# Attention with a gated unit: q and k transposes ahead of each burst's scores, casts and loads further ahead, last tokens in another burst, diagonals on VectorE

## The chip, the cores and the metric

The kernel runs on one core of a Trainium2 chip. The metric is the device time of one launch in microseconds (us), as the median of several runs; smaller is better. A profiled execution gives a span (first to last instruction) and a time of its own, which is a little longer than the span.

## The reference

Batch 8, 8 heads, 576 tokens, head dimension 64; all inputs are float32. Causal attention works in blocks of 64 tokens, and its output goes through a gated unit with a causal convolution of five taps:

```python
scores = scale * np.matmul(q, k.transpose(0, 1, 3, 2))      # scale = 1/8
scores = np.where(block_i >= block_j, scores, -1000000000.0)
attn = exp(scores - max); attn = attn / (sum + 1e-09)
x = matmul(attn, v), heads side by side                       # [8, 576, 512]
gate = sigmoid(sum over k of conv_w[k] * x shifted by 4 - k tokens)
out = (gate * (x @ w_val)) @ w_out                            # [8, 576, 512] float32
```

## The kernel before

Two heads of a batch make a pair; there are 32 pairs, four to a batch. The 576 tokens of a head are 512 "first" tokens and 64 "last" tokens (the tails). The order of all instructions is written out by hand (a manual schedule), so each engine works through its queue in the order of the program. The names in the profile are those of the tiles.

**Per pair.** `load_qk` (L101) puts q and k of a pair into the tile `kqst` through the queue of SyncE (SP); a pool `ld` of four buffers holds them. `cast_qk` (L134) makes float16 of them (tile `ckq`, four buffers), for all but the first pairs as one operation on GpSimd (POOL, L139). `trans` (L155) turns them with 16 small TensorE transposes into two PSUM banks (`ps_tr`, L163), and four copies of 128x256 carry these to `kT` and `qT` (L170, L173): three on VectorE (DVE) and one on ScalarE (ACT) from pair 8 on, two and two before. Column block 8 of `kT` is a copy of block 6 (L179). `scores` (L200) makes one of three chunks of a pair in a PSUM tile `S` of two banks, of which there are two; `exps` (L230) takes the exponential on ScalarE into `pt` (L232, 1.03 us), and for chunks 1 and 2 a copy and memsets on GpSimd follow (L235, L239, L242). `pv` (L256) multiplies with v (`ps_o`), and VectorE divides by the sums (L282, L284). `xt_pair` (L289) transposes the result (`ps_xt`, L296).

**The tails.** The q and k of a batch's last tokens are loaded for all 8 heads (`load_tails`, L114), cast (`cast_tails`, L144, tile `ct`), and transposed by `trans_tails` (L183, `ps_tt`) into `kX` and `qX`, which the scores of all four pairs of that batch read.

**The gated unit.** `gate` (L300) makes the convolution as TensorE products with diagonal matrices (`ps_gate`; `make_diag` L570 builds the 16 diagonals), with the last taps on VectorE (L312, and L327 in `end_gates`, L323) and a tanh on ScalarE (L319, L330). `val` (L333, `ps_val`) and `out_tile` (L356, `ps_out`, evicted by ScalarE at L367) are spread over the iterations by `filler` (L590), which takes work units from a list by fixed costs.

**PSUM.** Besides the two score tiles there are four banks, given out in turn (`bank`, L92) to `ps_tr`, `ps_tt`, `ps_o`, `ps_xt`, `ps_gate`, `ps_val`, `ps_out`. A piece of TensorE work that gets a bank waits until the piece four before it has been evicted.

**The loop** (L613) takes two pairs at a time, a and z = a + 1, in 16 iterations. Each has three bursts, each with two score chunks: (a,0) and (a,1); then (a,2) and (z,0); then (z,1) and (z,2). After the first burst come pv of the pair before and filler, after the second pv(a, part 0), after the third pv(a, part 1); gates and filler stand behind each. `j` is 0 or 2: an iteration with j = 0 has the first two pairs of a batch, j = 2 the last two. Bursts two and three also transpose pairs a + 2 and z + 2: in `burst` (L244) the scores come first, then `trans`, then the exponentials, with the last of the copies (the one on ScalarE) behind the first exponential:

```python
made = [(p, c, scores(p, c)) for p, c in chunks]
left = trans(ahead) if ahead < NP else None
if tails_of < B:
    trans_tails(tails_of)
```

Pair a + 2 is cast behind the first burst and pair z + 2 behind the second; each is transposed one burst later. The tails of the next batch are loaded at the start of an iteration with j = 0, cast behind the second burst of the one with j = 2, and transposed in its third burst.

Of the kernel before, what the change touches and what calls it, by code (L numbers as in the profile page):

```python
# [16 lines left out]
def kernel(  # L17
# [10 lines left out]
    nc = tc.nc  # L28
    fp32 = mybir.dt.float32
    fp16 = mybir.dt.float16  # L30
    AF = mybir.ActivationFunctionType
    ALU = mybir.AluOpType
    PSUM = bass.MemoryType.PSUM

    B, H, SEQ, D = q.shape
    NP = B * H // 2
# [11 lines left out]
    def const(shape, dtype, name):  # L48
        return cpool.tile(shape, dtype, tag=name, name=name)

    ident = const([128, 128], fp32, "ident")
    ident16 = const([128, 128], fp16, "ident16")
# [3 lines left out]
    convT = const([128, 4, 5], fp32, "convT")  # L56
    diag = const([128, 4, 4, 128], fp16, "diag")
# [19 lines left out]
    xts = [const([128, 4, PAD + SEQ], fp16, f"xt{i}") for i in range(2)]  # L77

    fast = ExitStack()
    ld = fast.enter_context(tc.tile_pool(name="ld", bufs=4))  # L80
    ldt = fast.enter_context(tc.tile_pool(name="ldt", bufs=2))
    wk = fast.enter_context(tc.tile_pool(name="wk", bufs=3))
    mo = fast.enter_context(tc.tile_pool(name="mo", bufs=6))
# [8 lines left out]
    def bank(name, dtype=fp32):  # L92
        return psM.tile([128, 512] if dtype == fp32 else [128, 1024], dtype,
                        tag="misc", name=name)
# [3 lines left out]
    FIRST = 8  # L98
# [21 lines left out]
    def load_v(p):  # L120
        b = p // PPB
        vs[p] = ld.tile([128, 2, 4, 64], fp32, tag="v", name="vst")
        for e in range(2):
            h = 2 * (p % PPB) + e
            nc.sync.dma_start(
                out=vs[p][:, e, :, :],
                in_=v[b, h, 0:512, :].rearrange("(t p) d -> p t d", p=128))
# [6 lines left out]
    def cast_qk(p, hows):  # L134
        t = c16[p] = wk.tile([128, 2, 4, 2, 64], fp16, tag="ckq", name="ckq", bufs=4)
        src = raw.pop(p)
        to = t[:, :, :, :, :].rearrange("p i t e d -> p i e t d")
        if len(hows) == 1:
            hows[0](out=to, in_=src[:, :, :, :, :])  # L139
        else:  # L140
            for i, how in enumerate(hows):
                how(out=to[:, i], in_=src[:, i, :, :, :])  # L142

    def cast_tails(b, how):  # L144
        t = tails[b] = wk.tile([128, 8, 64], fp16, tag="ct", name="ct", bufs=2)
        how(out=t[:, :, :], in_=tails32.pop(b)[:, :, :])

    def cast_v(p):
        nc.gpsimd.tensor_copy(out=ves[p % NV][:, :, :, 0:64], in_=vs.pop(p)[:, :, :, :])  # L149
# [5 lines left out]
    def trans(p):  # L155
        src = c16.pop(p)
        ps = [bank("ps_tr", fp16) for _ in range(2)]
        for i in range(2):
            for t in range(4):
                for r in range(2):  # L160
                    h = slice(64 * r, 64 * r + 64)
                    a = 256 * i + 64 * t
                    nc.tensor.transpose(out=ps[r][:, a:a + 64], in_=src[h, i, t, :, :],  # L163
                                        identity=ident16[h, h])

        def evict(i, r, copy):
            dst = (kTs[p % NT][:, 0:8, :], qTs[p % NT][:, :, :])[i]
            got = ps[r][:, 256 * i:256 * i + 256]
            if p < FIRST:
                copy(out=dst[:, 4 * r:4 * r + 4, :].rearrange("p n (s t) -> p (n s) t", t=4),  # L170
                     in_=got.rearrange("p (t s) -> p s t", t=4))
            else:
                copy(out=dst[:, r:8:2, :], in_=got.rearrange("p (t x) -> p t x", x=64))  # L173

        K = kTs[p % NT]
        evict(0, 0, nc.vector.tensor_copy)
        evict(0, 1, nc.vector.tensor_copy)
        copy = nc.vector.tensor_copy if p < FIRST else nc.gpsimd.tensor_copy
        copy(out=K[:, 8, :], in_=K[:, 6, :])  # L179
        evict(1, 0, nc.scalar.copy if p < FIRST else nc.vector.tensor_copy)  # L180
        return lambda: evict(1, 1, nc.scalar.copy)

    def trans_tails(b):  # L183
        src = tails.pop(b)
# [15 lines left out]
    def scores(p, c):  # L200
        ps = psS.tile([128, 2, 512], fp32, tag="S", name="S")
        b, j = divmod(p, PPB)
        K, Q = kTs[p % NT], qTs[p % NT][:, :, :].rearrange("p n x -> p (n x)")
        kx, qx = kXs[b % 2][:, j, :, :], qXs[b % 2][:, j, :]

        def group(off, lhsT, rhs, start=True, stop=True):
            n = rhs.shape[-1]
            for e in range(2):
                r = slice(64 * e, 64 * e + 64)
                mm(out=ps[:, e, off:off + n], lhsT=lhsT[r, :, :], rhs=rhs[r, :],  # L210
                   start=start, stop=stop)

        if c == 0:
            group(0, K[:, 0:2, :], Q[:, 0:512])
        elif c == 1:
            group(0, K[:, 2:4, :], Q[:, 128:512])

            group(384, K[:, 8:10, :], Q[:, 384:448], stop=False)
            group(384, kx, qx, start=False)
            group(448, K[:, 6:8, :], Q[:, 448:512])  # L220
        else:
            group(0, K[:, 4:6, :], Q[:, 256:512])
            for tt in range(4):
                group(256 + 64 * tt, K[:, 2 * tt:2 * tt + 2, :], qx)
        return ps
# [16 lines left out]
            nc.gpsimd.memset(seg[:, :, :, 0:64], 0.0)  # L242

    def burst(chunks, ahead=NP, tails_of=B):  # L244
        made = [(p, c, scores(p, c)) for p, c in chunks]
        left = trans(ahead) if ahead < NP else None
        if tails_of < B:
            trans_tails(tails_of)
        for p, c, s in made:
            exps(p, c, s)  # L250
            if left:
                left()
                left = None
        end_gates()

    def pv(p, part):  # L256
# [294 lines left out]
    load_v(1)  # L551
    load_qk(3)
    load_v(2)

    def load_weights():
        nc.gpsimd.dma_start(out=w_val_sb[:, :, :],
# [12 lines left out]

    def make_diag(g):  # L570
        for j in range(4):
            nc.scalar.activation(out=diag[:, g, j, :], in_=ident16[:, :], func=AF.Copy, bias=0.0,
                                 scale=convT[:, g, j:j + 1])

# [23 lines left out]

    pool = nc.gpsimd.tensor_copy
    cast_qk(0, (nc.vector.tensor_copy, nc.scalar.copy))
    cast_tails(0, nc.vector.tensor_copy)
    cast_qk(1, (nc.vector.tensor_copy, pool))
    cast_v(0)
    cast_vtails(0)
    cast_qk(2, (pool,))
    cast_v(1)
    trans(0)()
    trans_tails(0)  # L610
    trans(1)()

    for a in range(0, NP, 2):  # L613
        z = a + 1
        b, j = divmod(a, PPB)
        if a + 4 < NP:
            load_qk(a + 4)
        if a + 3 < NP:
            load_v(a + 3)
        if j == 0 and b + 1 < B:  # L620
            load_vtails(b + 1)
            load_tails(b + 1)
        flush()

        burst([(a, 0), (a, 1)])
        if 0 < a < NP - 2:
            cast_qk(a + 2, (pool,))
        if a:
            pv(z - 2, 0)
            filler(0.6)  # L630
            pv(z - 2, 1)
            xt_pair(a - 2)
        if a == 4:

            xt_pair(z - 2)
            for p in (a - 2, z - 2):
                gate(p, 0)
                gate(p, 1)
            end_gates()
            vals, outs = units(0)  # L640
            for _, work in vals:
                work()
            fill.extend(outs)
            weights[:] = [8.0]
            spent[0] = 0.0
        if a == 0:
            transpose_conv()
            make_diag(0)
            make_diag(1)
        filler(1.4)  # L650

        burst([(a, 2), (z, 0)], a + 2)
        if z + 4 < NP:
            load_qk(z + 4)
        if z + 3 < NP:
            load_v(z + 3)
        flush()
        if a and a != 4:
            xt_pair(z - 2)
        if z + 2 < NP:  # L660
            cast_qk(z + 2, (pool,))
        if a + 2 < NP:
            cast_v(a + 2)
        if j == 2 and b + 1 < B:
            cast_tails(b + 1, pool)
        pv(a, 0)
        if a > 4:
            if j == 0:
                vals, outs = units(b - 1)
                fill.extend(vals + outs)  # L670
                weights[:] = [8.0]
                spent[0] = 0.0
        if a == 0:
            load_weights()
            make_diag(2)
        filler(0.6)
        if a and a != 4:
            gate(a - 2, 0)
            gate(a - 2, 1)
        filler(0.6)  # L680

        burst([(z, 1), (z, 2)], z + 2, b + 1 if j == 2 else B)
        if z + 2 < NP:
            cast_v(z + 2)
        pv(a, 1)
        if j == 2 and b + 1 < B:
            cast_vtails(b + 1)
        if a == 0:
            make_diag(3)
        filler(0.4)  # L690
        if a and a != 4:
            gate(z - 2, 0)
            gate(z - 2, 1)
        filler(0.4)
# [62 lines left out]
```

## Time and profile before

| | |
|---|---|
| median of 3 runs | 222.28 us (222.24 to 222.92) |
| the profiled execution | 220.88 us, span 218.8 us |
| TensorE busy | 184.5 us (84%) |
| VectorE / ScalarE / GpSimd busy | 157.4 / 150.2 / 99.4 us |
| mean granted TensorE clock | 0.983 |

In the timeline a row gives the start and the length in us, the engine, the line and the operation with its tiles; in square brackets stands how long the engine had been idle before it and what ended that. "PEld" is the weight load of TensorE, "SPq" the queue of SyncE, on which loads and stores are issued.

### The profile page before, as it was taken

What the parts mean: (1) busy time and instruction counts of PE and PEld (TensorE: products, weight loads), DVE (VectorE), ACT (ScalarE), POOL (GpSimd) and SP (SyncE); (2) the same over time, 40 slices, a digit from 0 to 9 for tenths busy, and PEclk for the clock granted to TensorE, in tenths of its full rate; (3) what the DMA queues carried; (4) which work ended last, traced back from release to release, by engine and by line L of the source; (5) the groups of instructions that cost most, each with busy time, mean ns of one, the idle gap of its engine ahead of it and who ended that gap; (6) DMA issues with size and microseconds to landing.
All of it is one profiled execution on the core that took longest, in us unless ns stands there. A gap on an engine that the chain in (4) does not pass through costs nothing.

```text
span 218.8 us, 7511 instructions
## 1 busy us (share of the span) xinstructions
PE 184.5 (84%) x2946; PEld 128.4 (59%) x2946; DVE 157.4 (72%) x457; ACT 150.2 (69%) x227; POOL 99.4 (45%) x216
## 2 busy tenths in 40 slices
PE   1447889959688998999899989998999899998990
PEld 0335666745556756576567655675577566765740
DVE  3633468844687969698869876998699686989840
ACT  3299487269784868786887669768866887875420
POOL 4257446033745654647464554637455545410000
PEclk9999999988999999999999999999999999999996
DMA  5999998993988977997798887978799312001233
GB/s 154 266 290 151 230 293 170 198 229 100 232 194 206 234 163 210 251 209 160 184 264 208 183 236 181 236 172 202 198 265 213 100 65 100 0 37 62 100 135 115
DMA packets 107794, 39.36 MB, mean 180 GB/s; under 512 B 98021, under 2 KB 103141, under 8 KB 107754
## 3 DMA queue, kind: packets, MB, share of 16 engines
q1 hardware_dynamic: 106554, 37.51, 69.4%
q0 software_dynamic: 1056, 1.05, 3.2%
q8 instruction: 25, 0.41, 0.8%
q10 hardware_dynamic: 144, 0.26, 0.3%
q14 instruction: 15, 0.12, 0.2%
HBM read 30.42 MB, written 9.44 MB: 182 GB/s over the span
## 4 chain that ended last, share of the span: by engine, by line
PE 46%; DVE 16%; ACT 10%; issue 7%; DMA 7%; POOL 6%; SPq 6%; POOLq 0%; DVEq 0%; ACTq 0%
PE ps_val L43 10%; PE ps_out L43 10%; PE ps_gate L43 8%; PE ps_o L43 7%; PE S L43 6%; ACT pt L232 5%; DVE kT L173 4%; PE ps_tr L163 3%; DMA kqst<-in_k_dram 3%; POOL ckq L139 3%; DVE xn L284 3%; DVE th L327 3%; SPq L111 3%; DMA kqst<-in_q_dram 3%; ACT qT L170 2%
## 5 line engine op out<-in xcount | busy, mean ns | idle before, releaser
L232 ACT ACTIVATE pt<-S 128x1024 f16<-128x1024 f32 x96 | 96.6, 1027 | 21.8 <-PE S L43 21.4
L43 PE MATMUL ps_o<-ve,pt 128*128 128x65 f16 x896 | 39.8, 198 | 4.3 <-DVE qT L173 3.3
L43 PE MATMUL ps_val<-xt,w_val 128*128 128x288 f16 x256 | 37.6, 286 | 2.3 <-DVE qT L173 1.7
L43 PEld LDWEIGHTS <-pt 128*128 128x128 f16 x896 | 34.5, 101 | 7.5 <-DVE qT L173 3.9
L43 PE MATMUL ps_out<-w_out,gv 128*128 128x512 f16 x144 | 36.4, 385 | 0.8 <-DVE qT L173 0.8
L43 PE MATMUL S<-qT,kT 64*128 64x64 f16 (+3 forms) x320 | 31.8, 288 | 6.1 <-ACT pt L232 6.1
L367 ACT ACTIVATE ob<-ps_out 128x512 f32<-128x512 f32 x34 | 20.3, 598 | 20.1 <-PE ps_out L43 19.1
L284 DVE TENSOR_TENSOR xn<-ps_o,rinv 128x256 f16<-128x256 f32 x64 | 31.4, 491 | 2.2
L312 DVE SCALAR_TENSOR_TENSOR th<-xt,convT,ps_gate 128x288 f32<-128x288 f16 x64 | 30.2, 508 | 3.1 <-PE ps_gate L43 3.0
L43 PEld LDWEIGHTS <-kT 64*128 64x128 f16 x576 | 18.5, 98 | 23.7 <-issue 21.4
L139 POOL CAST ckq<-kqst 128x1024 f16<-128x1024 f32 x30 | 31.1, 1038 | 2.5 <-DMA kqst<-in_q_dram 0.7
L43 PE MATMUL ps_gate<-xt,diag 128*128 128x288 f16 x204 | 31.1, 291 | 0.9 <-DVE qT L173 0.8
L235 POOL COPY pd<-pt 64x128 f16<-64x128 f16 x32 | 12.8, 399 | 38.0 <-ACT pt L232 32.8
L43 PEld LDWEIGHTS <-w_val 128*128 128x128 f16 x256 | 23.0, 97 | 9.7 <-DVE qT L173 2.4
L344 DVE SCALAR_TENSOR_TENSOR gv<-th,ps_val 128x288 f16<-128x288 f32 x64 | 27.7, 449 | 1.0 <-PE ps_val L43 0.3
L173 DVE COPY kT<-ps_tr 128x256 f16<-128x256 f16 x48 | 11.7, 286 | 19.5 <-PE ps_tr L163 19.4
L43 PEld LDWEIGHTS <-diag 128*128 128x128 f16 x204 | 19.2, 99 | 7.3 <-DVE qT L173 1.2
L163 PE MATMUL ps_tr<-ident,ckq 64*128 64x64 f16 x512 | 14.5, 199 | 10.3 <-DVE ckq L142 4.1
L327 DVE SCALAR_TENSOR_TENSOR th<-xt,convT,th 128x576 f32<-128x576 f16 x26 | 21.2, 815 | 0.3
L43 PEld LDWEIGHTS <-gv 128*128 128x128 f16 x144 | 13.4, 99 | 12.7 <-DVE qT L173 1.2
L149 POOL CAST ve<-vst 128x512 f16<-128x512 f32 x32 | 19.6, 614 | 2.3 <-DMA vst<-in_v_dram 1.3
L242 POOL MEMSET pt<- 64x256 f16 x32 | 9.8, 306 | 22.3 <-ACT pt L232 20.6
(61 smaller groups left out, 204.4 us busy)
## 6 DMA issues: line engine op xcount, KB each, us to landing
out_dram<-ob SPq DMA_DIRECT2D x35, 256.0 KB, 3.3
vst<-in_v_dram SPq DMA_DIRECT2D x64, 128.0 KB, 3.2
kqst<-in_k_dram SPq DMA_DIRECT2D x48, 128.0 KB, 3.0
kqst<-in_q_dram SPq DMA_DIRECT2D x48, 128.0 KB, 3.2
kqst<-in_k_dram SPq DMA_DIRECT2D x8, 256.0 KB, 5.0
kqst<-in_q_dram SPq DMA_DIRECT2D x8, 256.0 KB, 5.2
t<-in_k_dram SPq DMA_DIRECT2D x8, 128.0 KB, 3.7
t<-in_q_dram SPq DMA_DIRECT2D x8, 128.0 KB, 3.6
```

The costliest lines, as they stand in the source:

```text
L43: nc.tensor.matmul(out=out, lhsT=lhsT, rhs=rhs, start=start, stop=stop, skip_group_check=True)
L139: hows[0](out=to, in_=src[:, :, :, :, :])
L149: nc.gpsimd.tensor_copy(out=ves[p % NV][:, :, :, 0:64], in_=vs.pop(p)[:, :, :, :])
L163: nc.tensor.transpose(out=ps[r][:, a:a + 64], in_=src[h, i, t, :, :], identity=ident16[h, h])
L173: copy(out=dst[:, r:8:2, :], in_=got.rearrange("p (t x) -> p t x", x=64))
L232: nc.scalar.activation(out=pt[:, :, 512 * c:512 * c + 512], in_=ps[:, :, :], func=AF.Exp, bias=0.0, scale=0.125)
L235: nc.gpsimd.tensor_copy(out=pds[p % NPT][64:128, 0:128].rearrange("p (e x) -> p e x", e=2), in_=pt[64:128, :, COL[3]:COL[3] + 64])
L284: nc.vector.tensor_tensor(out=x.rearrange("p c (e d) -> p (c e) d", e=2), in0=og[:, :, 0:64], in1=ri.to_broadcast([128, n, 64]), op=ALU.mult)
L312: nc.vector.scalar_tensor_tensor(out=th, in0=xts[b % 2][:, g, s0 + 4:s0 + 4 + HALF], scalar=convT[:, g, 4:5], in1=gp[:, 0:HALF], op0=ALU.m ...
L327: nc.vector.scalar_tensor_tensor(out=th, in0=xts[b % 2][:, g, 3:3 + SEQ], scalar=convT[:, g, 3:4], in1=th, op0=ALU.mult, op1=ALU.add)
L344: nc.vector.scalar_tensor_tensor(out=gvs[u][:, g, SEQ * bi + s0:SEQ * bi + s0 + HALF], in0=ths[b][:, g, s0:s0 + HALF], scalar=1.0, in1=vp[ ...
L367: nc.scalar.activation(out=ob[:, :], in_=ps[:, :], func=AF.Copy, bias=0.0, scale=0.5)
```

## The change

`trans` is issued ahead of the burst's scores, and all four copies out of it follow at once (no copy is kept for after the first exponential); for pairs from 8 on VectorE's order is k, q, k. The copy of block 6 of `kT` becomes a function of its own, `copy_key`, on GpSimd from pair 2 on, issued behind the burst. Pair z + 2 is cast behind the first burst, pair a + 4 behind the third. Loads run one pair further ahead, with five buffers. The tails of the next batch are cast behind the third burst of the iteration with j = 0, and transposed at the head of the first burst of the iteration with j = 2. The 16 diagonals are made on VectorE. In the prologue the first pair is transposed right behind its cast, the second pair behind the first burst.

```diff
-    ld = fast.enter_context(tc.tile_pool(name="ld", bufs=4))
+    ld = fast.enter_context(tc.tile_pool(name="ld", bufs=5))
...
+        evict(0, 0, nc.vector.tensor_copy)
+        evict(1, 0, nc.scalar.copy if p < FIRST else nc.vector.tensor_copy)
+        evict(0, 1, nc.vector.tensor_copy)
+        evict(1, 1, nc.scalar.copy)
+
+    def copy_key(p, how):
         K = kTs[p % NT]
-        evict(0, 0, nc.vector.tensor_copy)
-        evict(0, 1, nc.vector.tensor_copy)
-        copy = nc.vector.tensor_copy if p < FIRST else nc.gpsimd.tensor_copy
-        copy(out=K[:, 8, :], in_=K[:, 6, :])
-        evict(1, 0, nc.scalar.copy if p < FIRST else nc.vector.tensor_copy)
-        return lambda: evict(1, 1, nc.scalar.copy)
+        how(out=K[:, 8, :], in_=K[:, 6, :])
...
     def burst(chunks, ahead=NP, tails_of=B):
-        made = [(p, c, scores(p, c)) for p, c in chunks]
-        left = trans(ahead) if ahead < NP else None
+        if ahead < NP:
+            trans(ahead)
         if tails_of < B:
             trans_tails(tails_of)
-        for p, c, s in made:
+        for p, c, s in [(p, c, scores(p, c)) for p, c in chunks]:
             exps(p, c, s)
-            if left:
-                left()
-                left = None
         end_gates()
...
+    load_qk(4)
...
-            nc.scalar.activation(out=diag[:, g, j, :], in_=ident16[:, :], func=AF.Copy, bias=0.0,
-                                 scale=convT[:, g, j:j + 1])
+            nc.vector.tensor_scalar(out=diag[:, g, j, :], in0=ident16[:, :],
+                                    scalar1=convT[:, g, j:j + 1], scalar2=None, op0=ALU.mult)
...
     cast_qk(0, (nc.vector.tensor_copy, nc.scalar.copy))
+    trans(0)
+    copy_key(0, nc.vector.tensor_copy)
     cast_tails(0, nc.vector.tensor_copy)
+    trans_tails(0)
     cast_qk(1, (nc.vector.tensor_copy, pool))
+    cast_qk(2, (pool,))
     cast_v(0)
     cast_vtails(0)
-    cast_qk(2, (pool,))
-    cast_v(1)
-    trans(0)()
-    trans_tails(0)
-    trans(1)()
...
-        if a + 4 < NP:
-            load_qk(a + 4)
+        if a + 5 < NP:
+            load_qk(a + 5)
...
-        burst([(a, 0), (a, 1)])
-        if 0 < a < NP - 2:
-            cast_qk(a + 2, (pool,))
+        burst([(a, 0), (a, 1)], tails_of=b + 1 if j == 2 else B)
+        if a == 0:
+            trans(1)
+            copy_key(1, nc.vector.tensor_copy)
+        if z + 2 < NP:
+            cast_qk(z + 2, (pool,))
+        if a == 0:
+            cast_v(1)
...
         burst([(a, 2), (z, 0)], a + 2)
-        if z + 4 < NP:
-            load_qk(z + 4)
+        if a + 6 < NP:
+            load_qk(a + 6)
...
-        if z + 2 < NP:
-            cast_qk(z + 2, (pool,))
         if a + 2 < NP:
             cast_v(a + 2)
-        if j == 2 and b + 1 < B:
-            cast_tails(b + 1, pool)
+            copy_key(a + 2, pool)
         pv(a, 0)
...
-        burst([(z, 1), (z, 2)], z + 2, b + 1 if j == 2 else B)
+        burst([(z, 1), (z, 2)], z + 2)
+        if a + 4 < NP:
+            cast_qk(a + 4, (pool,))
         if z + 2 < NP:
             cast_v(z + 2)
+            copy_key(z + 2, pool)
+        if j == 0 and b + 1 < B:
+            cast_tails(b + 1, pool)
         pv(a, 1)
```

## The prediction

> **What bounds the kernel now.** I read the page's slices first, then the waits of TensorE, then the timeline of one period, engine by engine. The slices:
>
> ```profile
> PE   1447889959688998999899989998999899998990
> PEclk9999999988999999999999999999999999999996
> ```
>
> TensorE is short of work at the start and around 46 us, full behind that. What it waits for (total, times, longest):
>
> ```profile
> PE S L43 <- ACT pt L232: 6.1, 9, 1.6
> ...
> PE ps_o L43 <- DVE qT L173: 3.3, 5, 0.7
> PE ps_tr L163 <- POOL ckq L139: 3.2, 3, 1.3
> ```
>
> The first and third fall before 69.4 us. The second is a PSUM bank: work behind the transposes waits until the bank of `ps_tr` is evicted. With the same wait of `ps_val`, `ps_gate` and `ps_out` (1.7, 0.8, 0.8 us) it makes 6.6 us in all. From 69 us the kernel repeats every 46.0 us (two batches); the stretches by engine (length, then busy PE, PEld, DVE, ACT, POOL, then the clock):
>
> ```profile
> 44.10:47.50 3.40, 1.08 (x33) 0.83 (x30) 1.45 (x5) 2.70 (x5) 1.07 (x2) 1.00 0.97 223
> 47.50:50.90 3.40, 3.40 (x53) 2.50 (x53) 1.69 (x5) 1.97 (x4) 1.38 (x4) 0.53 0.76 167
> 64.50:67.90 3.40, 1.81 (x33) 1.26 (x33) 1.85 (x8) 2.15 (x4) 2.30 (x6) 1.00 0.99 253
> 92.57:138.58 46.01, 43.00 (x734) 29.89 (x736) 37.63 (x109) 35.21 (x49) 25.18 (x52) 1.00 0.84 208
> ```
>
> So a period leaves TensorE 3.0 us idle, all that any reordering can win there. GpSimd is busy for only 25 of 46 us, but in series. Its row around the tails' cast (`ct`):
>
> ```profile
> 101.81 0.31 POOL L242 MEMSET pt<- 64x256 f16 x1
> 102.18 1.04 POOL L139 CAST ckq<-kqst 128x1024 f16<-128x1024 f32 x1
> 103.16 0.62 POOL L149 CAST ve<-vst 128x512 f16<-128x512 f32 x1
> 103.72 0.62 POOL L146 CAST ct<-t 128x512 f16<-128x512 f32 x1
> ```
>
> The memset waits for an exponential, and three casts follow in queue order. Today the transposes of these tails come a burst later, and even so TensorE has waited for them once:
>
> ```profile
> 59.39 0.29 PE L189 MATMUL ps_tt<-ident,ct 64*128 64x64 f16 x8 [0.71 <-POOL ct L146]
> ```
>
> **The tails' new place: the term that decides.** With j = 0, behind the third burst, GpSimd's queue will hold: memsets of (z,1) and (z,2), the cast of pair a+4, the cast of v, `copy_key`, and last `ct`. The very next burst, the first with j = 2, has the tails' transposes at its head, ahead of its scores. From the end of exponential (z,2) the chain, start to start by the rows above, is 0.05 to the memset, 0.37 memset, 0.98 cast, 0.56 v, 0.3 `copy_key`, 0.62 `ct`, 0.05 to TensorE: 2.95 us. Against that stands how late (z,2) is. Two kinds of batch alternate; the tighter one before:
>
> ```profile
> 115.29 0.95 DVE L344 SCALAR_TENSOR_TENSOR gv<-th,ps_val 128x288 f16<-128x288 f32 x2
> 116.59 0.49 DVE L173 COPY kT<-ps_tr 128x256 f16<-128x256 f16 x2 [0.35 <-PE ps_tr L163]
> ...
> 117.11 0.37 ACT L173 COPY qT<-ps_tr 128x256 f16<-128x256 f16 x1
> 117.38 1.03 ACT L232 ACTIVATE pt<-S 128x1024 f16<-128x1024 f32 x1
> ...
> 118.48 0.58 PE L43 MATMUL S<-qT,kT 64*128 64x512 f16 x6
> ```
>
> Exponential (z,2) ends at 118.41 and TensorE reaches the next burst at 118.48: 0.07 us of slack, so a gap of 2.9 us if nothing else moved. But the copy on ScalarE waits for VectorE's copies of the same bank, and it now stands ahead of both exponentials, behind three copies of VectorE (0.75 us) that wait for the two `gv` (to 116.24): 116.24 + 0.75 + 0.4 + two exponentials 1.95 + latency = 119.4. The gap is about 4 us. In the other kind (third burst 92.50, next burst 96.25) the exponential ends 95.31 before and about 95.95 after, while TensorE comes about 0.5 earlier: gap 2.0 to 3.25 us.
>
> What comes back: the bank waits (0.29 four times, 0.62 and 0.70 a period) are covered by the scores, which now lie between the transposes and the next user of the bank. Part of that turns up elsewhere: transposes at the head of a burst need banks evicted that scores did not, and where ScalarE's `ob` copies stand behind late exponentials I find 0.3 to 1.0 us of new wait in three bursts of six. Walking the rows through a period, a tight batch loses 3.6 net (1.4 if everything comes back and (z,2) is not late; 4.05 if nothing comes back), the other 2.0 (0.5 to 3.25). Behind 69 us there are three tight ones (bursts now at 72.64, 118.48, 164.5) and two others (96.25, 142.3): 3 x 3.6 + 2 x 2.0 = **+14.8 us**.
>
> **The first pair and the diagonals.** The transposes of pair 0 no longer wait behind VectorE's casts, so the first exponentials start near 7.4 instead of 10.76, and ScalarE loses 16 x 409 ns of diagonals (2.44 of it directly ahead of an exponential at 15.16). On VectorE a diagonal lies between a 128x64 copy (182 ns) and a 128x320 tensor_scalar (327 ns): 2.9 to 5.2 us, taken 4, hidden in its idle times of 2.69, 2.61 and 1.89 us; without that cover `kT` copies come up to 0.5 later. But pair 2 still lands at 12.25, and its transposes now hold back the scores behind them: next exponential near 15.1, a gain of nothing; the third burst gains 1.1. Then the first burst of a = 2 has the tails of batch 1 at its head. Their loads are issued at 15.34 and 16.17 and land near 21; the load of pair 5 (0.5 MB) now goes ahead of them on SP's queue, as it does of v, so 22.8 to 24.5, and GpSimd's `ct` behind it. TensorE stands from 19.4 to about 24, where it started at 20.28 before, and then has no more waits for `ckq` (0.84), `ct` (0.32) and exponentials until a = 4. I take **+0.9** at 33.76 (-0.6 to +3). Loads further ahead cost nothing later: casts wait for DMA only before 13 us.
>
> **From a = 4 to 67 us.** The casts a burst earlier remove 1.03 and 1.32 of `ckq`, 0.71 of `ct`, about 1 of the 2.6 us for exponentials; the first burst of a = 6 gets a gap of 3.3 of the kind above. By rows, TensorE reaches the `ps_val` of 67.45 some **1.8 us** earlier (4 earlier to 0.5 later). Moved `copy_key` costs nothing: its reader is an iteration away. The end behind 184 us has neither transposes nor tails: 0.
>
> **The clock.** 32% busy in 44.1 to 47.5 was followed by half clock for 3.4 us; 53% in 64.5 to 67.9 was not. Half clock there took 3.52 us (16 transposes, a `pv`, an `out`) for what takes 2.03 elsewhere: 1.5 us. A gap of 4 us can leave a stretch that empty, one of 3 only by luck of the phase. I take two thirds of three drops in effect, partly covered: **+2.0** (0 to 7.5).
>
> [...]
>
> **Sum.** 0.9 - 1.8 + 14.8 + 2.0 = +15.9 on the profiled execution's 220.88: 236.8. The median of the runs stands 1.4 above that execution: 238.2, say **238.0 us**.
>
> **The rivals.** Forecast: 50%.
>
> [...] 20%.
>
> *The gaps are small*: (z,2) comes no later, all bank waits come back, and the start breaks even: 3 x 1.4 + 2 x 0.5 - 2 = +3.2, so 225.5. For it: VectorE is idle 0.35 ahead of its copies at 116.59. Against it: that idle is shorter than what the third copy adds. 20%.
>
> *Faster*: GpSimd delivers `ct` before TensorE arrives. Then the bank waits (6.6, less 1.5 of new ones), 1.8 at a = 4 to 8 as well as its 3.3 of gap come back, less the 0.9 of the start: 5.1 + 1.8 + 3.3 - 0.9 = 9.3, of which I leave 2.5 to VectorE, 1.97 of 2 us busy in 118 to 124: about 215.5. It needs the chain of 2.95 us to fit into less than 1.5 us a batch, the 3.0 of a period shared by two; at 0.07 and 0.94 us of slack I see nothing that shortens it, unless the casts run ahead of the memsets, which the queue forbids. 7%. Same: 3%, a mixture of small gaps and a good start.
>
> A difference of 0.3% (0.7 us) is about what a measurement of this kernel can tell from none. Faster 0.07, same 0.03, slower 0.90. The range takes in the small gaps' neighbourhood and three full clock drops with late banks (+22): 226 to 244; everything lost (3 x 4.05 + 2 x 3.25, 3, 0.5, 7.5: 251) is left out.
>
> **What would show it.** Right: `ps_tt <- POOL ct` as the largest wait of TensorE, some 20 us in seven waits, the ones from a = 10 on of 3 to 4 us; no bank wait behind `qT` copies; `ckq` gone from TensorE's waits; half-clock stretches behind the gaps; ScalarE's first exponential near 7.4. Wrong: `ct` waits under 1.5 us each, or the sum of the other waits of TensorE as large as before.

## The result, and the profile after

The changed kernel takes 241.38 us in the median of its first four runs (236.94 to 242.94), against 222.47 beside it, a ratio of 1.073 (95% interval 1.059 to 1.087). Run again later as E12, it takes 238.81 (235.38 to 244.25, six runs) against 222.41: 1.060 (1.055 to 1.065). It is slower by 6 to 7%. Ratios here leave out executions more than 1.5% above a kernel's fastest; of the changed kernel these are the ones with the lowest granted clock (0.925 to 0.946, the others 0.946 to 0.970), so a difference of medians that involves it is some 3 us larger than one by the ratios.

The first profile is of the execution of 242.94 us: span 241.1, where before had 218.8 (220.88). The two slice rows that were shown of before:

```profile
PE   1452498957995899959994999959994999998990
PEclk9999999997999799967999599967999799999997
```

TensorE, which was at 9 nearly everywhere behind a third of the span, now has a 4 or 5 once in every batch, and the clock row a 5, 6 or 7 in that slice or the one behind it. Its waits (total, times, longest):

```profile
PE ps_tt L190 <- POOL ct L146: 26.8, 7, 7.6
...
PE ps_tr L163 <- POOL ckq L139: 3.9, 2, 3.3
PE S L43 <- ACT pt L233: 2.4, 4, 0.9
```

The first row is new, and larger than all waits on banks that were gained: the 6.6 us of waits behind VectorE's `qT` are all gone from the list, and the wait of the scores for exponentials fell from 6.1 to 2.4. Here is one such stand, GpSimd first. Its columns are start, duration, engine and line:

```profile
102.46 0.31 POOL L243 MEMSET pt<- 64x256 f16 x1 [0.36 <-ACT pt L233]
102.83 1.04 POOL L139 CAST ckq<-kqst 128x1024 f16<-128x1024 f32 x1
103.81 0.61 POOL L149 CAST ve<-vst 128x512 f16<-128x512 f32 x1
104.36 0.24 POOL L182 COPY kT<-kT 128x64 f16<-128x64 f16 x1
104.54 0.61 POOL L146 CAST ct<-t 128x512 f16<-128x512 f32 x1
```

and TensorE at the end of it:

```profile
105.21 0.39 PE L190 MATMUL ps_tt<-ident,ct 64*128 64x64 f16 x8 [2.91 <-POOL ct L146]
```

Five instructions in a row, released by the exponential that ended at 102.34: 2.87 us from there to TensorE's start, and TensorE had run out of work 0.04 us earlier. The seven waits are 7.65 us at a = 2, 3.11 at a = 6, then 3.41, 2.91, 3.40, 2.91, 3.40. From its drop at 56.65 us on, each stretch between two changes of the granted clock in this profile lasts 3.413 us or a multiple of it: at half clock 3.41 (56.65 to 60.06) or 6.83 (104.43 to 111.26), at full clock 20.48 (111.26 to 131.74) or 47.8 (189.77 to 237.55). Cut along this raster, the stretches (length, PE busy with the number of instructions, granted clock, DMA share, GB/s) show what follows:

```profile
101.02:104.43 3.41, 1.29 (x11) 1.00 1.02 229
104.43:107.85 3.42, 2.64 (x31) 0.50 1.01 222
107.85:111.26 3.41, 3.41 (x38) 0.50 0.83 184
111.26:114.67 3.41, 3.41 (x55) 1.00 0.77 175
```

A stretch with TensorE busy for 1.29 us, then two at half clock: 38 instructions fill the second of these, and 55 the one behind it at full clock. The clock of this execution shows nine such half-clock stretches before its end, and that of before one (47.70 to 51.12).

The start has one stand of its own. GpSimd's cast waits not in its queue but for a transfer:

```profile
26.48 0.61 POOL L146 CAST ct<-t 128x512 f16<-128x512 f32 x1 [3.73 <-DMA t<-in_q_dram]
```

### The profile page after: what moved, and what is told of

It reads as the page before. It is cut to its first block, busy times and chain, and to the rows that moved or that the text cites. A ratio compares the mean times of both kernels' runs of the same rounds, so it can differ in the third digit from the quotient of the medians.

```text
span 241.1 us, 7534 instructions
## 1 busy us (share of the span) xinstructions
PE 191.2 (79%) x2946; PEld 133.2 (55%) x2946; DVE 161.8 (67%) x467; ACT 143.1 (59%) x211; POOL 97.5 (40%) x222
## 3 DMA queue, kind: packets, MB, share of 16 engines
q0 software_dynamic: 1056, 1.05, 2.8%
## 4 chain that ended last, share of the span: by engine, by line
PE 50%; DMA 14%; SPq 12%; ACT 6%; POOL 6%; DVE 4%; issue 3%; POOLq 0%; ACTq 0%; DVEq 0%
PE ps_val L43 11%; PE ps_out L43 10%; PE ps_o L43 10%; DMA vst<-in_v_dram 9%; PE S L43 7%; PE ps_gate L43 5%; SPq L111 5%; ACT pt L233 4%; DMA t<-in_q_dram 4%; PE ps_xt L292 3%; SPq L125 3%; PE ps_tr L163 2%; POOL ve L149 2%; SPq L107 2%; POOL ckq L139 2%
## 5 line engine op out<-in xcount | busy, mean ns | idle before, releaser
L233 ACT ACTIVATE pt<-S 128x1024 f16<-128x1024 f32 x96 | 93.5, 1033 | 29.0 <-PE S L43 29.0
L43 PE MATMUL ps_val<-xt,w_val 128*128 128x288 f16 x256 | 43.7, 313 | 0.0
L43 PE MATMUL ps_o<-ve,pt 128*128 128x65 f16 x896 | 42.9, 205 | 0.3 <-POOL pt L240 0.3
L43 PEld LDWEIGHTS <-pt 128*128 128x128 f16 x896 | 37.3, 105 | 4.6 <-POOL pt L240 1.0
L236 POOL COPY pd<-pt 64x128 f16<-64x128 f16 x32 | 9.4, 293 | 54.9 <-ACT pt L233 54.8
L43 PEld LDWEIGHTS <-w_val 128*128 128x128 f16 x256 | 25.7, 107 | 8.2 <-DVE xn L282 0.4
L173 ACT COPY qT<-ps_tr 128x256 f16<-128x256 f16 x24 | 8.9, 372 | 34.7 <-DVE kT L173 34.7
L190 PE MATMUL ps_tt<-ident,ct 64*128 64x64 f16 x64 | 2.9, 225 | 28.2 <-POOL ct L146 26.8
L163 PEld LDWEIGHTS <-ckq 64*128 64x128 f16 x512 | 10.8, 99 | 21.0 <-issue 5.2
L280 DVE RECIPROCAL rinv<-ps_o 128x4 f32<-128x4 f32 x64 | 11.8, 184 | 15.7 <-PE ps_o L43 14.8
```

Of the source, the lines that this page charges most:

```text
L43: nc.tensor.matmul(out=out, lhsT=lhsT, rhs=rhs, start=start, stop=stop, skip_group_check=True)
L233: nc.scalar.activation(out=pt[:, :, 512 * c:512 * c + 512], in_=ps[:, :, :], func=AF.Exp, bias=0.0, scale=0.125)
L236: nc.gpsimd.tensor_copy(out=pds[p % NPT][64:128, 0:128].rearrange("p (e x) -> p e x", e=2), in_=pt[64:128, :, COL[3]:COL[3] + 64])
L280: nc.vector.reciprocal(out=ri, in_=og[:, :, 64:65])
```

## The experiments

**Theory:** the tails' cast stands last in GpSimd's queue while their transposes stand first in TensorE's, so TensorE stands for the chain, and the half-clock stretches follow from the stands. **Rivals:** the new order of transposes and scores costs by itself; the clock falls without a price or without the stands; at the start it is the transfers.

**E1, the tails' cast ahead of the others** (on the changed kernel):

```diff
         burst([(z, 1), (z, 2)], z + 2)
+        if j == 0 and b + 1 < B:
+            cast_tails(b + 1, pool)
         if a + 4 < NP:
             cast_qk(a + 4, (pool,))
...
-        if j == 0 and b + 1 < B:
-            cast_tails(b + 1, pool)
```

> The changed kernel with one edit: the cast of the next batch's last tokens is put into GpSimd's queue right behind the third burst of a batch's first iteration, ahead of the cast of a pair, of the values and of the copy of the duplicate keys. Theory (the place in GpSimd's queue makes the wait): between the last exponential of the burst and the cast there is then only the memset (0.36 us) and the cast itself takes 0.61 to 0.62, so the chain is about 1.1 us instead of 2.95 (2.87 in the changed kernel's trace at the sixth pair of iterations), the waits of the tails' transposes shrink from 3.4 and 2.9 us by 1.8 to about 1.6 and 1.1, the one of the start (7.65, a transfer) stays, most of the five or six half-clock stretches between 56 and 190 us vanish: 6 x 1.8 = 11 us plus up to 9 x 1.5 of clock, so 225 to 229. The pair's and the values' casts come 0.6 us later, which nothing waits for. Rival (TensorE is held by something else, such as the late exponentials, and stands there whatever the queue does): within 3 us of the changed kernel's 237 to 242, the idle time only changing its name.

Measured: 220.67 us, 0.992 of before (0.988 to 0.996): below the 225 to 229 that were expected, and a little faster than before. GpSimd's row has the cast right behind the memset, and TensorE's wait has shrunk as foreseen (8.9 of the 16.7 at the start, then 0.4, and 1.69 and 1.19 in turn):

```profile
97.22 0.31 POOL L243 MEMSET pt<- 64x256 f16 x1 [0.36 <-ACT pt L233]
97.59 0.61 POOL L146 CAST ct<-t 128x512 f16<-128x512 f32 x1
```

```profile
PE ps_tt L190 <- POOL ct L146: 16.7, 7, 8.9
```

Two casts and a copy behind instead of ahead of one cast are worth 18 to 21 us by the medians, 15 to 18 by the ratios. Only one half-clock stretch is left (52.5 us). The place in the queue is the cause.

**E2, the transposes of the tails moved back** (on the changed kernel; the cast stays):

```diff
-        burst([(a, 0), (a, 1)], tails_of=b + 1 if j == 2 else B)
+        burst([(a, 0), (a, 1)])
...
-        burst([(z, 1), (z, 2)], z + 2)
+        burst([(z, 1), (z, 2)], z + 2, b + 1 if j == 2 else B)
```

> The changed kernel with one edit: the transposes of the next batch's last tokens go back into the third burst of the batch's second iteration (behind those of the pair), their cast stays at the end of the first iteration, so that it is a whole iteration ahead of them. All else of the change stays: transposes ahead of scores, casts and loads further ahead, diagonals on VectorE. Theory (the change loses only by the wait for the tails' cast and by the clock that it costs): no wait of the tails' transposes on GpSimd is left, the start's 7 us is gone too, no half-clock stretch but the one near 50 us or none; 241.4 minus 26.8 of waits minus some 10 of clock, plus what the shorter wait at the start uncovers: 212 to 219, faster than before's 222. Rival A (the transposes at a burst's head make the first exponential of each burst wait for VectorE's copies, and that costs time itself): 222 to 230, with ScalarE's waits of some 30 us behind the copies reappearing in TensorE's waits as S behind exponentials. Rival B (before was bound by TensorE's own work, and nothing is left to gain): 220 to 223.

Measured: 211.98 us, 0.953 (0.946 to 0.960). Without the new place of the tails' transposes the change is a gain of over 4%; rivals A and B fall. The wait for the tails' cast behind the start is gone, and two batches now take:

```profile
77.78:121.99 44.21, 42.79 (x744) 29.74 (x738) 39.83 (x108) 34.34 (x50) 25.51 (x52) 1.00 0.92 220
```

44.2 us against 46.0 before: of the 3.0 us that TensorE was idle in a period, 1.4 are left. At the start the tails' transfer still costs, by another way. GpSimd waits 4.6 us for it, and TensorE for a memset behind:

```profile
PE ps_o L43 <- POOL pt L240: 5.5, 2, 5.2
```

**E3, the tails' part alone** (on the kernel before): `trans_tails(b + 1)` ahead of the first burst at j = 2, `cast_tails` behind the third burst at j = 0.

> The kernel before with only the last tokens' part of the change: their cast goes behind the third burst of a batch's first iteration and their transposes ahead of the scores of the second iteration's first burst; transposes of pairs stay behind the scores, casts and loads stay where they were, diagonals stay on ScalarE. No pair's cast stands ahead of the tails' cast in that burst here, so the chain is 2.95 minus 0.98, about 2 us. Theory (the wait comes from the chain alone): seven waits of the tails' transposes on GpSimd, of some 2.4 in three batches and 1.9 in three, and 3 or more at the start (their transfer): 16, less what half of the hidden bank waits give back (2), plus up to four half-clock stretches (6): 229 to 238. Rival (the tails' place costs only together with the new order of transposes and scores): 221 to 224.

Measured: 226.02 us, 1.019 (1.012 to 1.027).

```profile
PE ps_tt L189 <- POOL ct L146: 11.3, 7, 3.2
```

That is between the two expectations and meets neither. The part costs alone, so it needs no new order. The waits behind the start are 2.1, then 1.5 and 0.7 in turn, shorter than I expected: 8.1 us in all, in a kernel that is 3.7 us slower, one half-clock stretch more than before included.

**E4, the stand filled with work** (on the changed kernel):

```diff
+        if b > 1:
+            fillbank = bank("ps_fill")
+            for _ in range(20):
+                mm(out=fillbank[:, 0:HALF], lhsT=w_val_sb[:, 0, 0:128], rhs=w_out_sb[:, 0, 0:HALF])
         ps = [bank("ps_tt", fp16) for _ in range(2)]
```

> The changed kernel with 20 products of 128x128 by 288 (weights, a bank that nothing reads) put ahead of the tails' transposes of batches 2 to 7, some 2.4 us of TensorE work at full clock, in the place where it stands 2.9 to 3.4 us. The output is the same. Theory (part of the loss is the clock that falls after each stand): the wait shrinks to about 0.5 to 1.0 us, the half-clock stretches behind 80 us vanish (nine windows of 3.413 us at half clock go to one or two), mean clock 0.98 or more instead of 0.93, and the time falls by 7 x 1.5 = 10 us at most, 5 at least, to 231 to 236, although TensorE has more to do. Rival (the stand alone costs, the clock is a follower without a price): 240 to 244, with the clock high or not.

Measured: 231.65 us, 1.043 (1.034 to 1.051). 120 needless products make the kernel 7 to 10 us faster than the changed one by the medians (4 to 7 by the ratios), because from 55 us to the end the clock never falls:

```profile
PEclk9999999997999999999999999999999999999996
```

This run separates the two costs. The real work still starts as late after each stand (the fill, 2.5 us each, since 40 products make TensorE 47.1 us busy in a period where E1 has 42.1, and 0.96 or 0.46 of wait), and two batches take 49.0 to 49.1 us: 3.1 more than before. In the changed kernel's first profile they take 54.6. The two periods, the changed kernel's first:

```profile
105.42:160.00 54.58, 47.75 (x741) 33.13 (x737) 38.99 (x108) 34.28 (x49) 23.92 (x52) 0.88 0.70 172
103.50:152.65 49.15, 47.13 (x776) 33.52 (x772) 37.97 (x109) 34.20 (x49) 23.93 (x52) 1.00 0.78 190
```

The 5.5 us between lie in four half-clock stretches: 1.4 us each.

**E5, the whole tails part undone** (on the changed kernel: E2, and the cast back at the end of the second burst at j = 2).

> The changed kernel with its whole tails part undone: the cast of the next batch's last tokens back at the end of the second burst of the batch's second iteration, their transposes back in the third. Against the run with the transposes alone moved back (211.98) only the cast moves, an iteration later. Theory (GpSimd's queue again: in that run the cast stood at the end of the first iteration and GpSimd waited 4.6 us for the tails' transfer until 27.8 us, with the zeroing of an exponential tile behind it, for which TensorE stood 5.2 us): that stand goes, some 4 of its 5.2 us are gained, 207 to 209. Rival (at the start the transfers bound all engines, whoever waits): 211 to 213.

Measured: 217.83 us, 0.982 (0.978 to 0.986). Both expectations missed: it is 6 us slower than E2. GpSimd's queue shows why; it wants the values of a later pair first:

```profile
31.36 0.61 POOL L149 CAST ve<-vst 128x512 f16<-128x512 f32 x1 [5.45 <-DMA vst<-in_v_dram]
31.91 0.24 POOL L182 COPY kT<-kT 128x64 f16<-128x64 f16 x1
32.09 0.61 POOL L146 CAST ct<-t 128x512 f16<-128x512 f32 x1
```

These values are issued at 20.59, behind a pair that is loaded further ahead than before, and take until 31.3; the tails' cast waits behind theirs although its own transfer is done. TensorE stands 6.23 us for it, up to 32.76, and the clock is at half from 28.5 to 38.8. Later it waits 1.0 to 1.7 for the tails in every other batch. It is the same fault in another place: a cast that TensorE needs next, queued behind one that it doesn't.

**E6, the order of transposes and scores undone too** (on E5: `made = scores` ahead of `trans(ahead)`, ScalarE's copy behind the first exponential).

> The same as the run beside it (tails part undone) with the order of pairs' transposes and scores undone too: transposes behind the scores, ScalarE's copy behind the burst's first exponential, as before the change. Left of the change: casts a burst ahead, loads further ahead, keys copied apart, diagonals on VectorE, the start. Theory (the order pays, because the transposes' banks are then free before the next products ask for a bank: TensorE's waits of 0.3 to 0.7 us for banks behind VectorE's copy of qT, 6.6 us in all before, are gone in every run with transposes ahead, and two batches take 44.2 us there against 45.9 before): 4 to 6 us slower than the run beside it, about 213. Rival (the casts ahead made the difference): within 1 us of it.

Measured: 220.64 us, 0.994 (0.991 to 0.998), 2.8 slower than E5. The order pays, by a little over half of what I expected; TensorE's waits for `ps_o` behind `qT` are back (3.0 us in six), and two batches take 45.2 instead of 44.7.

**E7, the tails' loads ahead** (on E1):

```diff
+        if j == 0 and b + 1 < B:
+            load_tails(b + 1)
         if a + 5 < NP:
             load_qk(a + 5)
         if a + 3 < NP:
             load_v(a + 3)
         if j == 0 and b + 1 < B:
             load_vtails(b + 1)
-            load_tails(b + 1)
```

> The run with the tails' cast ahead of the others in GpSimd's queue (220.67), with one more edit: the loads of the next batch's last tokens are issued ahead of those of a pair, of its values and of the values' last tokens, instead of behind them. Theory (the stand of 7.7 to 8.9 us at the start is the tails' transfer, issued at 16.9 and 18.1 us and landing near 27 because it queues behind 0.6 MB of others): issued 2 to 3 us sooner, the start's stand shrinks by 2 to 3, what it delays (a pair and values) is not needed before 30 us: 217.5 to 219. Rival (the transfer competes with the weights, 1 MB that GpSimd issues at 18 to 20 us, and lands when these land): 220 to 221.5.

Measured: 215.93 us, 0.975 (0.971 to 0.979), 4.7 less than E1, somewhat more than expected.

```profile
20.98 0.61 POOL L146 CAST ct<-t 128x512 f16<-128x512 f32 x1
```

The cast has no wait for a transfer left (in E1 it had 6.8 us of it), and TensorE's wait at a = 2 is 2.15 instead of 8.86. The stand of the start was the transfer's place on the DMA queue; the weights, issued as before, did not hold it.

**E8, diagonals on ScalarE again** (on E5).

> The run with the tails part undone, with the diagonals back on ScalarE. Theory (the diagonals are hidden where they are: VectorE makes 16 of them in 3.2 us between 11 and 21 us, while TensorE waits for casts and transfers, and ScalarE has room in the same stretch): within 0.7 us of it, either way. Rival (ScalarE is what the start's chain of exponentials hangs on, and 16 more instructions delay it): 1 to 3 us slower.

Measured: 218.64 us, 0.983 (0.980 to 0.987) against E5's 0.982: no difference that this shows.

**E9, E2 with the loads of E7.**

> The run with only the tails' transposes moved back (211.98) with the tails' loads issued ahead of the pair's and the values', as in the run at 215.93. Theory (the same transfer that costs the start there holds GpSimd for 4.6 us here, and TensorE behind it for 5.2): landing some 6 us sooner, as it did there (21.0 against 27.6 us), it holds nothing, the 5.2 us go, and the values' transfers are next late, by about 1 to 2: 207.5 to 210. Rival (the order with which GpSimd's casts meet the transfers only shifts the stand to the values' cast, as in the run with the whole tails part undone, where that wait was 5.45): 211 to 213, or above.

Measured: 212.19 us, 0.957 (0.952 to 0.961): nothing gained over E2, as the rival said. GpSimd no longer waits for the tails but for the values behind them, longest 5.0 us, near 31 us:

```profile
POOL ve L149 <- DMA vst<-in_v_dram: 6.5, 2, 5.0
```

**E10, E9 with the weights' loads later** (`load_weights()` from the first iteration's second burst to behind the second iteration's first).

> The run beside it with the two loads of weights (1 MB) issued by GpSimd in the second iteration's first burst (near 24 us) instead of at 18 to 20 us. Theory (all 16 DMA engines are busy from 8 to 32 us, so whatever of 1 MB is taken out of that stretch, some 4 us at 250 GB/s, brings the values' and pairs' transfers forward): the values' wait of GpSimd near 32 us goes, 1 to 2 us faster than the run beside it. Rival (the weights are then late for the first products with them near 36 us, since they took 7 and 10 us to land): 1 us or more slower.

Measured: 209.39 us, 0.940 (0.935 to 0.946), 2.8 less than E9, more than the 1 to 2 expected: the fastest, faster than both kernels. The half-clock stretch that E9 has at 33.5 us is gone too.

```profile
POOL ve L149 <- DMA vst<-in_v_dram: 2.3, 1, 2.3
```

**E11, the changed kernel with the loads of E7, and E12, the changed kernel again**, side by side.

> The changed kernel with one edit: the tails' loads issued ahead of the pair's, the values' and the values' tails. Theory (the start's stand of 7.65 us is the tails' transfer, and its price adds to that of the later stands): that stand shrinks to 2 to 3 us, as it did with the cast ahead (8.86 to 2.15, 220.67 to 215.93), and TensorE still stands 2.9 to 3.4 us in each later batch with its half-clock stretches: 4 to 6 us faster than the unedited changed kernel run beside it. Rival (the phase of the stands against the clock's windows decides, and moving all stands by 5 us shifts it): less than 3 or more than 8 us, with another number of half-clock windows than nine.

> The changed kernel unedited, for its clock in another execution: the runs of it so far span 236.94 to 242.94, and the profile is of the longest. Theory (stands of 2.9 to 3.4 us cost the same each time, the clock drops behind them vary with where they fall in windows of 3.413 us): the waits for the tails' cast again 19 us in six behind the start, a time below 242.9 goes with fewer than nine half-clock windows, about 1.4 us a window. Rival (the drops are a disturbance of that one execution): a profile near 237 with the stands and without drops behind 69 us.

Measured: E11 234.39 us, 1.049 (1.044 to 1.053), 4.4 less than E12 by the medians, 2.5 by the ratios, with the wait of the start 4.7 instead of 8.0. The two profiles are of nearly the same length (235.4 and 235.5 us) with seven half-clock stretches in E11's and five in E12's; at 1.4 us for a stretch E11 is 2.9 us shorter without the clock, which is about what the wait lost. So the sooner load is worth about 3 us here, less than the 4 to 6 expected, and the rest of the difference of medians is the number of drops, which differs from execution to execution. E12's profile is of an execution of 237.47 us (span 235.5), and its stands are the same as in the first profile, to 0.01 us behind the start:

```profile
PE ps_tt L190 <- POOL ct L146: 27.2, 7, 8.0
```

```profile
PEclk9999999997999799999999999979996799999998
```

It has five half-clock stretches instead of nine. 241.1 less 235.5 is 5.6 us, 1.4 for each of the four. E12's rival falls: the drops are no disturbance of one execution, though their number differs from one to the next.

## Why the prediction was right, and where not

The forecast of 238.0 and the mechanism hold: TensorE stands for the tails' cast, and the clock falls behind the stands. That the sum came so near is luck, since the stands' net was too large by 7 to 9 us, and the clock, the start and the part from a = 4 to a = 8 were too small by about as much in E12's execution (in the first profile's by 15). Measured against before's profile, in us, by TensorE's first scores of a = 8 (62.05 before) and its last `ps_xt` (200.20):

| term | predicted | first profile | E12's profile |
|---|---|---|---|
| start, to a = 4 (`ps_xt` at 36.40 before) | +0.9 | +3.5 | +3.1 |
| a = 4 to a = 8 | -1.8 | +1.0 | +0.9 |
| five stands behind it, without clock | +14.8 | about +6 | about +6 |
| clock drops behind it | +2.0 | 8 x 1.4 = +11.2 | 4 x 1.4 = +5.6 |
| the end | 0 | +0.6 | +0.9 |
| span | +15.9 | +22.3 | +16.7 |

The row of the stands is what is left of 17.2 and 11.8 us between the two marks when the clock is taken off. By the prediction's own marks (33.76 and 67.45) the first two rows read +2.9 and +0.1 (E12: +2.5 and 0.0), and the stands about +7.5.

**The chain** was right: 2.95 us predicted, 2.87 from exponential to transposes. The stands were 3.4 and 2.9, where I had 4 and 2.0 to 3.25, since the exponential comes about 0.5 us later than TensorE in the tight batches, not 1.05.

**The net of the stands was about twice what it is.** I took nearly all of a stand as lost (3.6 of 4). E4 shows a pair of them, 6.3 us raw, to cost 3.1 a period against the kernel before. What failed is the step "what comes back": without stands a period is 1.7 us shorter than before (E2), where I let new waits at the bursts' heads (0.3 to 1.0 in three bursts of six) eat most of it. The trace has three such waits in all, 1.4 us. And a stand is itself partly made up for: 44.2 plus 6.3 would be 50.5, and E4 takes 49.1.

**The clock was too small in its count, not in its price.** 1.5 us for a half-clock stretch was predicted, 1.4 measured. But I let only the stands of 4 us count, and those of 3 "only by luck of the phase". Of two stands of 2.91 us in E12 one brought a drop and the other none, but mostly it went against the kernel: of the ten stands of 2.9 and 3.4 us behind a = 8 in the two profiles eight brought a drop, and four of these cost two stretches. That the clock would hold (236.0, the forecast less its 2.0) falls, as E4 shows by making it hold: 231.65, with more work. No stand of 4 us was needed: 2.91 us were enough at a = 14 and a = 22 of the first profile, and E1's one drop came behind a stretch in which TensorE was never idle for more than 0.87 us (49.03 to 52.45).

**The start** failed in one step: the tails of batch 1 landing at "22.8 to 24.5". They landed just ahead of 26.5, their q half 8.6 us after its issue, where before it took 4.8: I had moved the issue past pair 5's load and left the transfer at its old length. "Loads further ahead cost nothing later" was wrong in the same way, as the values' waits in E5 and E9 show (5.45 and 5.0 us, where before's longest was 1.3); that the loads further ahead are their cause is read from the order of issue, since no run puts those loads back alone. **From a = 4 to a = 8** I expected a gain of 1.8; the waits for `ckq` did go, but the 3.11 us stand at a = 6 and the drop behind it, in place of before's one drop, took more than they gave.

**The small steps** held: no bank wait behind `qT` is left; the first exponential starts at 7.80 instead of 10.76; pair 2's cast holds the next scores; the diagonals on VectorE are hidden (3.2 us in all by the rows; E8). "`ckq` gone from TensorE's waits" is true behind 17 us only. The rival "faster" (215.5) needed the tails' cast in time: E2 gives it that, and 212.0.

## What to carry to other kernels

GpSimd worked through its queue as it was written (its rows from 102.46 to 104.54 in the changed kernel, from 97.22 to 97.59 in E1), so a cast belongs in it by when its reader comes: an engine busy for 40% of the span held the busiest one because the cast wanted next stood last, and moving it up by three places was worth 15 to 21 us (E1). Where a change puts a consumer at the head of one queue, look at what stands ahead of its producer in the other, waits for transfers included. And price a stand twice: as the time that does not come back (E4's period is 4.9 us longer than E2's, of 6.3 us of stands), and as the clock that falls behind it (1.4 us for each half-clock stretch here).

## What the runs showed of the hardware

The length of a stand alone did not tell whether the clock fell. In E12 two stands of 2.91 us, the one at a = 14 (from 101.79 to 104.70) and the one at a = 22 (from 150.91 to 153.82), lie differently to the raster of 3.413 us:

```profile
100.23:103.64 3.41, 1.56 (x13) 1.00 1.00 227
103.64:107.05 3.41, 2.35 (x57) 1.00 1.17 230
...
151.43:154.85 3.42, 1.02 (x26) 1.00 0.77 174
154.85:158.26 3.41, 3.41 (x38) 0.50 1.00 224
```

The first is split between two stretches, with 1.56 and 2.35 us of work, and nothing happens; the other leaves one stretch with 1.02 us, and half clock follows. In the first profile, from 53.24 to 220.49 us, six stretches at full clock were followed by half clock. TensorE was busy in them for 0.81, 1.26, 1.29, 0.70, 1.25 and 0.67 us, and in each other one at full clock for 2.16 or more. In before's profile, from 30.64 to 201.30 us, the one that half clock followed held 1.09 us (44.29 to 47.70), and each other one at full clock 1.87 or more.

Busy time alone does not part the two, though. In E1 a stretch with 2.01 us was followed by half clock, and one with 1.73 was not:

```profile
49.03:52.45 3.42, 2.01 (x58) 1.00 0.75 197
52.45:55.86 3.41, 3.00 (x26) 0.50 0.52 117
...
72.93:76.35 3.42, 1.73 (x31) 1.00 1.08 225
```

What else counts, no run shows. At half clock, three stretches of the first profile were followed by a second one, those with 2.64, 2.73 and 2.67 us behind the stands at a = 14, 18 and 22; the one with 2.75 (186.35 to 189.77) and those with 3.41 were followed by full clock.

In the first profile the half-clock stretches behind the stands at a = 14, 18, 22 and 26 begin at 104.43, 131.74, 159.05 and 186.35 us, 27.3 us apart, which is as long as the batches take there, and each of these stands brings its drop. E12 has batches of 24.5 and 24.6 us there, and no drop behind the stands at a = 14 and a = 18. That the drops hold themselves in step is the author's reading of these two executions, and no run shows it.
